# Attention and expert layer on one core: bias tables built from the first score maximum on, half of the last logits summed apart, and transfers that wait for a VectorE operation

## The chip, the core and the metric

The kernel runs on one core of one Trainium2 chip. A core has five engines: TensorE (PE, with its weight loads PEld), VectorE (DVE), ScalarE (ACT), GpSimd (POOL) and SyncE (SP). SP computes nothing here; it issues the DMA transfers, one after the other. The metric is the device time of one execution in microseconds (us), as the median of several runs.

## What is computed

Sliding-window attention with a distance bias for 8 batches of 8 heads, 576 positions and 64 columns, and behind it a layer of 8 experts in which each expert takes at most 80 of the 4608 tokens. Cut to what matters:

```python
# q, k, v: (8, 8, 576, 64)
rel = pos[:, None] - pos[None, :]
scores = q @ k.T / 8 + slope[head] * -abs(rel), where 0 <= rel < 128, else -1e9
attn = exp(scores - max);  x = attn / (sum(attn) + 1e-9) @ v          # tokens 4608 x 512
logits = x @ w_gate                                                  # 512 x 8
expert = argmax(logits);  gate = softmax(logits)[expert]
for e in range(8):                          # the 80 tokens with the largest gate
    out[tok] = gate[tok] * (relu(x[tok] @ w1[e]) @ w2[e])            # 512 x 1024, 1024 x 512
# every other row of out is zero
```

## The kernel before

The program has an attention part and an expert part. The attention part is recorded as operations, put in order by the class `Plan`, and only then issued. That is why nearly all its instructions carry one line, L346, the call in `issue`. `order` (L231) is a list scheduler: it keeps a clock for each engine, estimates each operation's cost, and takes on each engine the ready operation with the smallest key. The key is the place in the program plus the numbers of the table `SHIFT` (L23) for the operation's kind; `SLACK`, `PATIENCE` and `URGENT` say how far it looks ahead and how long TensorE stays in one tile shape. SP's transfers are ordered in the same way. On the chip each engine then runs its own list strictly in order, and waits on semaphores where data or a buffer is missing.

The attention part goes through 80 groups, 10 for each batch. For a group i the steps are: `scores` (TensorE writes the tiles s; VectorE adds the bias table, takes the row's extremum mn and writes e in one custom operation, followed by a read of its accumulator; ScalarE takes the exponential in place), `turned` one group later (TensorE transposes e into pt, VectorE or ScalarE copies it to ptb) and `attend` another group later (TensorE multiplies ptb with the values v into av). A third kind of value column holds a one, so that the last column of av is the sum that the row has to be divided by. `attended` (L781) copies av to xs in SBUF and, after every second pair of heads, writes xs to x_dram in HBM with two transfers.

The bias tables are bneg (tiles of full width), bn (the first tile of a row, masked) and bnx (tiles over two pairs of heads), each a product of a slope sl or slx and the distance rel plus the penalty pen. VectorE builds all of them with `add_bias` (L469) at the program's start. `load_pair` loads q and k of two heads into one of four buffers, `load_vt` a transposed copy of the values for the logits, `load_v` the values with their extra columns. `selection_constants` (L576) makes the tables that the merging below needs, in part on VectorE.

After each batch `merge_steps` (L839) picks the best 80 tokens for each expert among the batch and those kept so far: `norm` takes the reciprocal ztk of the sums, `gate` multiplies the value logits by it (lw), sums over the heads (lg), and goes on with maximum, exponential and selection; `parts` writes the matrix T (ts), `turn` transposes it to m_tp and copies two parts of it to sst (VectorE) and ttt (ScalarE); `diff`, `places` and `keep` (m_d, m_cs, m_gp) count who is ahead of whom. For the last batch nothing lies beside these steps but `keep_clock`, 100 small matmuls (idle_a) without use for the result. The batch in `FAST` does its small steps on VectorE rather than GpSimd.

The expert part is written in plain order. After 10 warm-up matmuls (`warm_up(10, "warm1")`, L1057) `gather` fetches 80 rows of x_dram for each expert, `turn` (L1099) divides them by the sums (rz), scales them by the gate and transposes them; two matrix products h and y follow for each expert. The weights of experts 0 and 1 are loaded during attention, as is the zeroing of out; the others follow the first gathers.

Of the kernel before, what the change touches and what calls it, by code (L numbers as in the profile page):

```python
# [18 lines left out]
P = 128  # L19
# [3 lines left out]
SHIFT = {"idle": 100000, "EXP": 5, "PTB": -45, "AV": 5, "PT": -15, "S": -50, "TTR": 60, "ADD": 80}  # L23
SLACK = 20.0
# [5 lines left out]
class Plan:  # L30
# [17 lines left out]
    DRAIN, PATIENCE, URGENT = 93.0, 150.0, 60  # L48
# [36 lines left out]
    def _labels(self, op, aps):  # L85
        if self.stage == "init":
            return []
# [61 lines left out]
    def add(self, ns_name, eng, name, args, kw):  # L149
# [24 lines left out]
        else:  # L174
            op = _Op(eng, len(self.ops), cost, call)
            op.issue = 450.0 if eng == "SP" and len(outs[0].ap) < 3 else 625.0
            op.lag = 70.0 if name == "tensor_tensor_reduce" else 0.0
# [53 lines left out]
    def order(self, free_order=()):  # L231
# [23 lines left out]
        mode, tick, cols, cold = None, 0, 0.0, True  # L255

# [14 lines left out]
        while len(done) < len(ops):  # L271
# [40 lines left out]
            o.start = t  # L312
            if e == "SP":
                o.end = dma = max(t + self.DMA, dma) + o.cost
                clock[e] = max(t + o.issue, dma - self.DMA)
            else:
                o.end = clock[e] = t + (2 * o.cost if e == "PE" and cold else o.cost)
            done.append(o)
# [22 lines left out]
    def issue(self, tc, free_order=()):  # L341
        done = self.order(free_order)
        with tc.manual_schedule():
            for o in done:
                for c in o.calls:
                    c.ins = c.f(*c.args, **c.kw)  # L346

# [27 lines left out]
def tile_attention_then_moe(  # L375
# [40 lines left out]

    def staged(label, f):
        def run():
            nc.stage = label
            f()  # L420
            nc.stage = None
        return run
# [49 lines left out]
    def make_bias(g):  # L472
        for a_ in range(2):
            add_bias(bneg[:, g, a_], sl[:, g, a_:a_ + 1], rel, pen)
        for a_ in range(2):
# [26 lines left out]
    def load_v(b):  # L502
        for g in range(0, NP, 2):
# [3 lines left out]
        nc.gpsimd.memset(vts[b % 2].rearrange("p g h n c -> p (g h n) c")[:, :, XW - 1:XW], 1.0)  # L507
# [17 lines left out]
    load_pair(0, 1)  # L525
    load_vt(0)
    wg = const.tile([P, NP, 32], F32, name="wg")
    nc.gpsimd.memset(wg, 0.0)
# [8 lines left out]
    load_v(0)  # L537
    load_pair(0, 2)
    nc.vector.memset(zero, 0.0)
# [34 lines left out]
    ztk = [persist.tile([P, NU, H], F32, name=f"ztk{i}") for i in range(2)]  # L574

    def selection_constants():  # L576
# [3 lines left out]
        nc.vector.tensor_copy(pf, pi)  # L580
# [3 lines left out]
        nc.vector.tensor_copy(uf, ui)  # L584
        pb = pf.broadcast_to([P, NU])
        for t in ts:
# [4 lines left out]
            nc.vector.tensor_scalar(t[:, :, 29], pb, EPS, None, ALU.mult)  # L591
            nc.vector.tensor_scalar(t[:, :, 30], uf, EPS, None, ALU.mult)
            nc.vector.tensor_scalar(t[:, :, KS + 27], pb, 0.5, -EPS, ALU.add, ALU.mult)
            nc.vector.tensor_scalar(t[:, :, KS + 28], uf, -EPS, None, ALU.mult)
        bi = const.tile([P, B, NU], I32, name="bi")
        nc.gpsimd.iota(bi, pattern=[[S, B], [P, NU]], base=P, channel_multiplier=0)
        nc.vector.tensor_copy(idc[:, :, 0], bi.rearrange("p b u -> p (b u)"))
        nc.vector.tensor_copy(idc[:, :, 1], pf.broadcast_to([P, B * NU]))
        ii = const.tile([P, R], I32, name="ii")
        nc.gpsimd.iota(ii, pattern=[[-1, R]], base=0, channel_multiplier=0)  # L600
        nc.vector.tensor_copy(itb, ii)
# [16 lines left out]
        nc.vector.tensor_copy(ita, ij)  # L618
        nc.vector.tensor_copy(identb, ident)
# [4 lines left out]
        nc.vector.tensor_copy(wt, wt_i)  # L624
        nc.vector.tensor_copy(wtu, wt.unsqueeze(1).broadcast_to([P, NU, 8]))
        nc.vector.memset(wtu[64:128, NU - 1], -1.0)
# [41 lines left out]
    def value_columns(b):  # L668
        def run():
            lp = ps(f"vw{b}")  # L670
            sel = ident.rearrange("p (g c) -> p g c", g=NP)
            with nc.together():
# [8 lines left out]
            nc.scalar.copy(  # L681
                vts[b % 2][:, :, :, :, D:D + E].rearrange("p g h n e -> p g (h n) e"),
                lp[:, 0:64 * NVP].rearrange("p (m g e) -> p g m e", g=NP, e=E))
# [19 lines left out]
    def scores(i, b, steps):  # L703
# [17 lines left out]
        for s, st in enumerate(steps):  # L721
# [4 lines left out]
            for a_ in range(2):  # L726
# [3 lines left out]
                nc.vector.tensor_tensor_reduce(  # L730
                    x, sps[a_][:, 192 * s + o0:192 * s + 192], bias, -(D ** -0.5), 3.0e38, ALU.add, ALU.min, m)
# [49 lines left out]
    def attended(b, g):  # L781
# [8 lines left out]
        if g % 2:  # L790
            r0, h0 = P + S * b, 2 * g - 2
            xd = x_dram.rearrange("r (h d) -> r h d", d=XW)
# [15 lines left out]
    def gate(b):  # L808
        ve = nc.vector if b in FAST else nc.gpsimd
        lg = small.tile([P, NU, E], F32, tag="lg", name=f"lg{b}")  # L810
        lw = small.tile([P, NU, H, E], F32, tag="lw", name=f"lw{b}")
        zt = ztk[b % 2]
        ve.tensor_tensor(lw, xss[b % 2][:, :, :, D:D + E], zt.unsqueeze(3).broadcast_to([P, NU, H, E]), ALU.mult)
        nc.vector.tensor_reduce(lg, lw.rearrange("p u h e -> p u e h"), axis=AX.X, op=ALU.add)
# [24 lines left out]
    def merge_steps(b):  # L839
# [5 lines left out]
        def parts():  # L845
# [26 lines left out]
            th = small.tile([P, 2, E], BF16, tag="th", name=f"th{b}")  # L872
            for j in range(2 if last else 1):
                ve.tensor_scalar(th[:, j], eq[:, j], 0.5, None, ALU.mult)
            st["th"] = th
# [3 lines left out]
        def turn():  # L879
            tp = psb(f"m_tp{b}")  # L880
            with nc.together():
                for u in range(NU):
# [349 lines left out]
```

## Time and profile before

| what | value |
|---|---|
| median of 3 runs (342.03 to 346.26) | 342.69 us |
| the profiled execution | 342.97 us |
| its span, first to last instruction | 341.2 us |
| mean granted TensorE clock | 0.962 |
| attention part, to the end of the last av | 0 to 227.97 us |
| selection of the last batch, to the first token numbers (gid) | 228.04 to 240.49 us |
| first expert's h to the last y | 246.77 to 335.44 us |
| bytes moved | 98.09 MB |

The profile is one execution, so a sum made from it is held against 342.97 us. Its times count from the span's start. PE matmuls overlap, so that a busy TensorE is not one at its peak; idle time of an engine costs only where that engine is the one that others wait for. "issue" as a releaser means that the engine waited for nothing that the profile shows.

### The profile page before, as it was taken

Reading aid. Unit: us, or ns where it says so; the run is one execution under the profiler, and the core shown is the slowest. Engines: PE = TensorE matmul, PEld = TensorE weight load, DVE = VectorE, ACT = ScalarE, POOL = GpSimd, SP = SyncE. Lnnn points to the kernel's source line nnn. Section 1 sums busy time; section 2 is a strip of 40 time slices with the busy share of each in tenths; the row PEclk is TensorE's granted clock in tenths of the full one; section 3 lists DMA queues with packets and bytes.
Section 4 is the critical chain, followed back from the end, with each engine's and each line's share of the span. In section 5 each row is a group of like instructions: output and inputs, shape, how many; then the busy total and the mean of one; then the engine's idle time right before and its main releaser. Section 6 shows DMA issues by size and latency. Waiting matters only on the chain. (4 is left out here: it accounts for less than half of the span.)

```text
span 341.2 us, 14662 instructions
## 1 busy us (share of the span) xinstructions
PE 310.1 (91%) x6069; PEld 243.9 (71%) x6069; DVE 194.1 (57%) x964; ACT 204.6 (60%) x554; POOL 59.5 (17%) x223
## 2 busy tenths in 40 slices
PE   7399999999999889996988999997679999999993
PEld 6278888888787778795877888896675566655660
DVE  8957667688767687876558787866400122210200
ACT  1469979789958869887576997963003222233221
POOL 7700012022012004013000401200540111100111
PEclk9699999999999999999699999999779999999998
DMA  6995979998989999999499999831299999999300
GB/s 195 343 409 184 345 257 302 355 318 297 349 301 314 318 324 273 337 338 340 134 295 314 315 391 338 326 133 52 75 306 355 399 402 400 395 397 401 133 21 19
DMA packets 44113, 98.09 MB, mean 287 GB/s; under 512 B 4240, under 2 KB 14224, under 8 KB 44048
## 3 DMA queue, kind: packets, MB, share of 16 engines
q1 hardware_dynamic: 43024, 94.36, 79.0%
q0 software_dynamic: 1024, 2.81, 2.7%
q8 instruction: 48, 0.79, 0.9%
q14 instruction: 17, 0.14, 0.1%
HBM read 75.34 MB, written 21.81 MB: 285 GB/s over the span
## 5 line engine op out<-in xcount | busy, mean ns | idle before, releaser
L346 ACT ACTIVATE e<-e,mn 128x192 f32<-128x192 f32 (+1 forms) x288 | 108.4, 437 | 16.0 <-DVE mn L346 15.7
L346 PE MATMUL av<-v,ptb 128*64 128x73 f32 (+1 forms) x2112 | 73.3, 232 | 6.1 <-issue 6.1
L346 PEld LDWEIGHTS av<-v,ptb 128*64 128x64 f32 (+1 forms) x2112 | 64.1, 135 | 17.0 <-issue 12.3
L346 DVE CUSTOM_DVE_ANT_0 e<-s,bneg 128x192 f32<-128x192 f32 x192 | 59.9, 350 | 9.0 <-PE s L346 6.0
L346 PE MATMUL pt<-ident,e 128*128 128x128 f32 x432 | 58.7, 284 | 3.6 <-DVE identb L346 3.6
L346 PE MATMUL s<-kp,q 64*64 64x192 f32 (+1 forms) x1152 | 58.3, 316 | 3.9 <-DVE mn L346 2.5
L346 PEld LDWEIGHTS pt<-ident,e 128*128 128x128 f32 x432 | 48.6, 145 | 10.7 <-POOL e L346 3.9
L346 DVE COPY ptb<-pt 128x384 f32<-128x384 f32 x80 | 43.0, 550 | 15.7 <-PE pt L346 10.3
L1177 DVE TENSOR_TENSOR ys<-ys,y 80x512 f32<-80x512 f32 x8 | 5.5, 684 | 77.6 <-ACT ys L1172 77.6
L346 PEld LDWEIGHTS s<-kp,q 64*64 64x64 f32 x1152 | 40.6, 134 | 8.5 <-issue 4.3
L1147 PEld LDWEIGHTS h<-xgTs,w 128*64 128x64 f32 x1024 | 40.0, 146 | 9.0 <-issue 8.9
L1147 PE MATMUL h<-xgTs,w 128*64 128x80 f32 x1024 | 41.9, 244 | 2.3 <-issue 2.3
L1170 PE MATMUL y<-w,hT 128*32 128x512 f32 (+1 forms) x288 | 42.8, 594 | 0.0
L346 ACT COPY xs<-av 128x584 f32<-128x584 f32 (+1 forms) x64 | 27.9, 462 | 15.3 <-PE av L346 14.0
L346 ACT COPY ptb<-pt 128x384 f32<-128x384 f32 x64 | 30.3, 474 | 8.9 <-PE av L346 4.4
L1170 PEld LDWEIGHTS y<-w,hT 128*32 128x32 f32 (+1 forms) x288 | 10.5, 105 | 24.9 <-issue 24.2
L1152 ACT ACTIVATE hT<-h 128x320 f32<-128x320 f32 x16 | 7.0, 437 | 35.5 <-PE h L1147 35.5
L346 DVE CUSTOM_DVE_ANT_0 e<-s,bn 128x128 f32<-128x128 f32 x64 | 16.1, 286 | 16.1 <-PE s L346 15.1
L346 DVE DVE_READ_ACCUMULATOR2_ANT mn<- 128x1 f32 x288 | 23.8, 82 | 0.0
L1180 POOL DMA_INDIRECT out_dram<-ys,sid x8 | 7.4, 921 | 78.9 <-DVE rz L1104 60.4
L346 DVE TENSOR_SCALAR_CACHE_REDUCE ncm<-m_d 128x80 bf16<-128x80 f32 (+5 forms) x55 | 17.2, 370 | 2.7 <-PE m_d L346 2.5
L346 POOL MEMSET e<- 128x128 f32 x32 | 6.5, 204 | 64.3 <-PE pt L346 58.5
(143 smaller groups left out, 352.0 us busy)
## 6 DMA issues: line engine op xcount, KB each, us to landing
w<-in_moe_w_dram SPq DMA_DIRECT2D x64, 512.0 KB, 10.8
v<-in_v_dram SPq DMA_DIRECT2D x16, 730.0 KB, 6.2
x_dram<-xs SPq DMA_DIRECT2D x16, 584.0 KB, 4.4
l_vt<-in_vt_dram SPq DMA_DIRECT2D x16, 576.0 KB, 7.3
out_dram<-zero SPq DMA_DIRECT2D x18, 512.0 KB, 6.7
kp<-in_k_dram SPq DMA_DIRECT2D x31, 288.0 KB, 4.6
q<-in_q_dram SPq DMA_DIRECT2D x31, 288.0 KB, 6.6
x_dram<-xs SPq DMA_DIRECT2D x16, 73.0 KB, 5.0
```

Of the source, the lines that this page charges most:

```text
L346: c.ins = c.f(*c.args, **c.kw)
L1147: nc.tensor.matmul(hp[64 * hh:64 * hh + 64, R * fi:R * fi + R], lhsT=a[:, cc, f0:f0 + 64], rhs=xgT[:, cc], start=(cc == 0), stop=(cc == NC ...
L1152: nc.scalar.activation(hT[:, 4 * f2:4 * f2 + 4].rearrange("p c r -> p (c r)"), hp[:, 0:4 * R], AF.Relu)
L1170: nc.tensor.matmul(o, lhsT=hT[:, f_, l0:l1], rhs=c[:, f_], start=st, stop=sp)
L1177: nc.vector.tensor_tensor(ys, ys, yp[0:R, 0:DM], ALU.add)
L1180: nc.gpsimd.indirect_dma_start(out=out, out_offset=bass.IndirectOffsetOnAxis(ap=sid[:, e:e + 1], axis=0), in_=ys, in_offset=None, bounds_c ...
```

## The change

Five things change together.

1. The planner's numbers are others (`SHIFT`, `SLACK`, `PATIENCE`, `URGENT`), and so the order on every engine. Operations of the new stage "bias" get the kind I and no shift.
2. Each transfer of the attention part that the plan puts after 14 us gets an extra dependence: SP waits for the last VectorE operation that, by the plan, has ended 0.3 us before.
3. At the start only bneg of the first pair is built ahead of the scores. The other tables follow one by one behind the first score maximum, the selection constants behind group 4 and on GpSimd alone. The gate matrix wg comes padded from the host in one transfer instead of two scattered ones, half of the values is loaded ahead of the second pair of q and k, and the value columns of batch 0 are copied in two halves.
4. The sums are inverted in place in xs for each half of the heads, ahead of the write to x_dram. So the expert part needs no rz. For the last batch the first half's logits are summed while attention still runs, the second half's after it, and the two are added. `turn` of the last batch transposes T twice, into m_tp and m_tq, so that the two copies read different tiles; the halves th are taken in `turn` rather than in `parts`.
5. `warm_up` ahead of the experts has 17 matmuls instead of 10.

```diff
-SHIFT = {"idle": 100000, "EXP": 5, "PTB": -45, "AV": 5, "PT": -15, "S": -50, "TTR": 60, "ADD": 80}
-SLACK = 20.0
+SHIFT = {"idle": 100000, "EXP": 45, "E": 60, "PTB": 15, "TTR": -20, "AV": 15, "M": 60, "S": 35, "XS": -80, "PT": 20}
+SLACK = 0.0
...
+    PACED = 14000.0
+    DRAIN, PATIENCE, URGENT = 93.0, 50.0, 100
...
+            if e == "SP" and t > self.PACED:
+                while len(beat) > 1 and beat[1].end + self.LAT["DVE"]["SP"] <= t:
+                    beat.pop(0)
+                o.pace = beat[0]
...
+                if o.pace is not None:
+                    tc.add_manual_dep(
+                        o.calls[0].ins.ins, o.pace.calls[-1].ins.ins.name,
+                        mybir.DependencyInfo(mybir.DependencyClass.Sync, mybir.DependencyReason.DATA),
+                        reason="a short queue")
...
+    make_bias(0)
     nc.vector.tensor_copy(pen0, pen[:, 64:192])
     nc.vector.memset(pen0[0:64, 0:64], -BIG)
-    make_bias(0)
...
     load_pair(0, 0)
-    load_pair(0, 1)
     load_vt(0)
...
-    for hh in range(2):
-        nc.sync.dma_start(
-            out=wg[64 * hh:64 * hh + 64, :, 8 * hh:8 * hh + 8],
-            in_=w_gate.rearrange("(g hh p) e -> hh p g e", g=NP, hh=2)[hh],
-        )
+    nc.sync.dma_start(out=wg.rearrange("p g c -> p (g c)"), in_=w_gate)
...
-    load_v(0)
+    load_v(0, 0)
+    load_pair(0, 1)
+    load_v(0, 1)
     load_pair(0, 2)
-    nc.vector.memset(zero, 0.0)
...
-        nc.vector.tensor_copy(uf, ui)
+        nc.gpsimd.tensor_copy(uf, ui)
...
-    def norm(b):
-        zt = ztk[b % 2]
+    def norm(b, h0):
         ve = nc.vector if b in FAST else nc.gpsimd
-        ve.tensor_scalar_add(zt, xss[b % 2][:, :, :, XW - 1], 1.0e-9)
-        nc.vector.reciprocal(zt, zt)
+        x = xss[b % 2][:, :, h0:h0 + 4]
+        z = x[:, :, :, XW - 1]
+        with at_stage(f"n{b}"):
+            ve.tensor_scalar_add(z, z, 1.0e-9)
+            nc.vector.reciprocal(z, z)
+
+    def logits(b, h0, n):
+        ve = nc.vector if b in FAST else nc.gpsimd
+        x = xss[b % 2][:, :, h0:h0 + n]
+        lg = small.tile([P, NU, E], F32, tag="lg", name=f"lg{b}_{h0}", bufs=3)
+        lw = small.tile([P, NU, n, E], F32, tag="lw", name=f"lw{b}_{h0}")
+        ve.tensor_tensor(
+            lw, x[:, :, :, D:D + E], x[:, :, :, XW - 1:XW].broadcast_to([P, NU, n, E]), ALU.mult)
+        nc.vector.tensor_reduce(lg, lw.rearrange("p u h e -> p u e h"), axis=AX.X, op=ALU.add)
+        lgs.setdefault(b, []).append(lg)
...
+        logits(b, 4 if b in FAST else 0, 4 if b in FAST else H)
+        lg = lgs[b][-1]
+        if len(lgs[b]) > 1:
+            nc.vector.tensor_tensor(lg, lg, lgs[b][0], ALU.add)
...
-            tp = psb(f"m_tp{b}")
+            tp = tq = psb(f"m_tp{b}")
+            for o in range(2 if last else 1):
+                if o:
+                    tq = psb(f"m_tq{b}")
...
-            for g in range(1, NP):
-                make_slopes(g)
-            for u in range(2):
-                make_cross_slopes(u)
-            make_bias(1)
-            make_cross_bias(0)
...
+            later.extend((
+                lambda: make_start_bias(0), lambda: (make_cross_slopes(0), make_cross_bias(0)),
+                lambda: (make_slopes(1), make_bias(1)), lambda: make_start_bias(1),
...
+                lambda: nc.gpsimd.memset(zero, 0.0)))
+            with nc.after(first[0]):
+                staged("bias", later.pop(0))()
+        for _ in range(2):
+            if later and i:
+                with nc.after(first[0]):
+                    staged("bias", later.pop(0))()
+        if i == 4:
+            with nc.after(first[0]):
+                staged("bias", selection_constants)()
...
-        warm_up(10, "warm1")
+        warm_up(17, "warm1")
...
-        nc.vector.tensor_scalar_add(rz, xg[:, :, XW - 1], 1.0e-9)
-        nc.vector.reciprocal(rz, rz)
```

What this does to the order is shown at three places; the number behind an underscore tells buffers apart. First VectorE at the start. ISA is the custom operation that writes e and mn from a tile s, and behind it the read of the accumulator. Before, these are the last tables and the first maximum:

```order
L346 SCALAR_TENSOR_TENSOR bneg<-rp,sl 128x192 x2
L346 SCALAR_TENSOR_TENSOR bn_84<-rp,sl 128x128 x2
L346 SCALAR_TENSOR_TENSOR bnx<-rp,slx 128x192 x2
L346 ISA e_129,mn_130<-s_0_131,bneg 128x192
L346 ISA mn_130 128x1
```

Now, from the penalty on:

```order
L355 TENSOR_SCALAR rp<-rp_i 128x192
L355 SCALAR_TENSOR_TENSOR bneg<-rp,sl 128x192 x2
L355 COPY rp<-rp 128x128
L355 MEMSET rp 64x64
L355 ISA e_127,mn_128<-s_0_129,bneg 128x192
L355 ISA mn_128 128x1
```

Nine pairs of table operations and a memset of zero have moved from ahead of the first maximum to behind it.

Second SP in the middle of the attention part, at the transfers that follow the second half of batch 5 (xs_120 is its result, v_92 the values of batch 6 or 7, w a piece of expert 1). The brackets name what an instruction waits for: DMAHW is an earlier transfer on the same ring. Before:

```order
L346 DMA x_dram<-xs_120 128x4x292 [waits DMAHW5_49,Activation_49]
L346 DMA x_dram<-xs_120 64x292 [waits DMAHW6_49,Activation_49]
L346 DMA v_92<-in_v_dram 128x1460 [waits DMAHW7_49,PE_49]
L346 DMA kp_89<-in_k_dram 128x576 [waits DMAHW0_49,PE_49]
L346 DMA q_1_688<-in_q_dram 128x576 [waits DMAHW1_49]
L346 DMA kp_90<-in_k_dram 128x576 [waits DMAHW2_49,PE_49]
L346 DMA q_2_715<-in_q_dram 128x576 [waits DMAHW3_49]
L346 DMA w_1_128<-in_moe_w_dram 128x2x512 [waits DMAHW4_49]
```

Now:

```order
L355 DMA v_92<-in_v_dram 128x1460 [waits DVE_49,DMAHW2_49,PE_49,Pool_49]
L355 DMA x_dram<-xs_120 128x4x292 [waits DMAHW3_49,DVE_49,Activation_49]
L355 DMA x_dram<-xs_120 64x292 [waits DMAHW4_49,DVE_49,Activation_49]
L355 DMA kp_88<-in_k_dram 128x576 [waits DMAHW5_49,DVE_49,PE_49]
L355 DMA q_0_668<-in_q_dram 128x576 [waits DMAHW6_49,DVE_49]
L355 DMA kp_89<-in_k_dram 128x576 [waits DMAHW7_49,DVE_49,PE_49]
L355 DMA q_1_687<-in_q_dram 128x576 [waits DMAHW0_49,DVE_49]
L355 DMA kp_90<-in_k_dram 128x576 [waits DMAHW1_49,DVE_49,PE_49]
L355 DMA q_2_718<-in_q_dram 128x576 [waits DMAHW2_49,DVE_49]
L355 DMA w_1_126<-in_moe_w_dram 128x2x512 [waits DMAHW3_49,DVE_49]
```

The run of transfers is as long as before, but each has a VectorE operation of its own to wait for, and the values come ahead of the write of xs.

Third VectorE behind the last av, where xs_121 is the last batch's result. Before:

```order
L346 TENSOR_SCALAR ztk_124<-xs_121 128x40
L346 RECIPROCAL ztk_124<-ztk_124 128x40
L346 TENSOR_TENSOR lw_935<-xs_121,ztk_124 128x320
L346 TENSOR_REDUCE lg_934<-lw_935 128x40
L346 TENSOR_REDUCE mx_936<-lg_934 128x5
```

Now:

```order
L355 TENSOR_SCALAR xs_121<-xs_121 128x5x4
L355 RECIPROCAL xs_121<-xs_121 128x5x4
L355 TENSOR_TENSOR lw_4_935<-xs_121 128x160
L355 TENSOR_REDUCE lg_4_934<-lw_4_935 128x40
L355 TENSOR_TENSOR lg_4_934<-lg_4_934,lg_0_898 128x40
L355 TENSOR_REDUCE mx_936<-lg_4_934 128x5
```

The first four operations work on half as many elements, and one addition comes between the sum and the maximum. The halves th stay where they were in VectorE's list, ahead of kk.

More of the change, by code (lines that the diff above doesn't have):

```diff
@@ L317, in order @@
                 o.end = clock[e] = t + (2 * o.cost if e == "PE" and cold else o.cost)
+            if e == "DVE":
+                beat.append(o)
             done.append(o)
@@ L415, in tile_attention_then_moe, with at_stage @@
     x_dram = dram.tile([P + NTOK, H * XW], F32, name="x_dram")
+    @contextmanager
+    def at_stage(label):
+        old, nc.stage = nc.stage, label
+        yield
+        nc.stage = old
     def staged(label, f):
@@ L500, in tile_attention_then_moe, with load_v @@
     vtt = {}
-    def load_v(b):
-        for g in range(0, NP, 2):
+    def load_v(b, half=None):
+        for g in range(0, NP, 2) if half is None else (2 * half,):
             nc.sync.dma_start(
@@ L617, in selection_constants @@
         nc.gpsimd.iota(ij, pattern=[[1, R]], base=0, channel_multiplier=-1)
-        nc.vector.tensor_copy(ita, ij)
-        nc.vector.tensor_copy(identb, ident)
+        nc.gpsimd.tensor_copy(ita, ij)
+        nc.gpsimd.tensor_copy(identb, ident)
         nc.gpsimd.memset(at, 0.0)
@@ L680, in run @@
                                 lhsT=lx[:, x:x + 64], rhs=sel[:, :, 8 * hh:8 * hh + 8], start=True, stop=True)
-            nc.scalar.copy(
-                vts[b % 2][:, :, :, :, D:D + E].rearrange("p g h n e -> p g (h n) e"),
-                lp[:, 0:64 * NVP].rearrange("p (m g e) -> p g m e", g=NP, e=E))
+            w = NP if b else NP // 2
+            for g in range(0, NP, w):
+                nc.scalar.copy(
+                    vts[b % 2][:, g:g + w, :, :, D:D + E].rearrange("p g h n e -> p g (h n) e"),
+                    lp[:, 0:64 * NVP].rearrange("p (m g e) -> p g m e", g=NP, e=E)[:, g:g + w])
         return run
@@ L729, in scores @@
                 x = e[:, s, a_, o0:]
-                nc.vector.tensor_tensor_reduce(
-                    x, sps[a_][:, 192 * s + o0:192 * s + 192], bias, -(D ** -0.5), 3.0e38, ALU.add, ALU.min, m)
+                first.append(nc.vector.tensor_tensor_reduce(
+                    x, sps[a_][:, 192 * s + o0:192 * s + 192], bias, -(D ** -0.5), 3.0e38, ALU.add, ALU.min, m))
                 nc.scalar.activation(x, x, AF.Exp, bias=m, scale=-1.0)
@@ L871, in parts @@
                 idc[:, NU * b:NU * b + NU].unsqueeze(3).broadcast_to([P, NU, 2, E]), ALU.mult)
[L872 to L875, printed above, removed]
             if last:
@@ L879, in turn @@
         def turn():
-            tp = psb(f"m_tp{b}")
-            with nc.together():
-                for u in range(NU):
-                    nc.tensor.transpose(tp[:, P * u:P * u + P], T[:, u], identb)
-                nc.tensor.transpose(tp[:, S:S + R], at, identb[0:R, 0:R])
-            nc.vector.tensor_copy(sT[0:KS], tp[0:KS, 0:NU * P])
+            tp = tq = psb(f"m_tp{b}")
+            for o in range(2 if last else 1):
+                if o:
+                    tq = psb(f"m_tq{b}")
+                with nc.together():
+                    for u in range(NU):
+                        nc.tensor.transpose(tq[:, P * u:P * u + P], T[:, u], identb)
+                    nc.tensor.transpose(tq[:, S:S + R], at, identb[0:R, 0:R])
             nc.scalar.copy(tT[0:KS], tp[KS:2 * KS, 0:S + R])
+            nc.vector.tensor_copy(sT[0:KS], tq[0:KS, 0:NU * P])
             st["a1"] = small.tile([P, 2], F32, tag="a1", name=f"a1_{b}")
             st["nc"] = ncm
+            th = small.tile([P, 2, E], BF16, tag="th", name=f"th{b}")
+            for j in range(2 if last else 1):
+                ve.tensor_scalar(th[:, j], st["eq"][:, j], 0.5, None, ALU.mult)
+            st["th"] = th
         def diff(pieces):
@@ L982, in tile_attention_then_moe @@
     nc.stage = None
+    later = []
+    first = []
     zeros = []
@@ L1003, in finish_group @@
             attended(b, g)
+            if b in FAST and g == 1:
+                staged(f"n{b}", lambda: logits(b, 0, 4))()
             if g == NP - 1:
@@ L1199, in _layout @@
     a['vt'] = a['vt'].transpose(0, 2, 1, 3).reshape(B, 128, -1)
+    w = a['moe_w_gate'].reshape(H // 2, 2, D, E).transpose(1, 2, 0, 3)
+    wg = _np.zeros((2, D, H // 2, 32), w.dtype)
+    for h in range(2):
+        wg[h, :, :, E * h:E * h + E] = w[h]
+    a['moe_w_gate'] = wg.reshape(128, -1)
     v = a['v'].reshape(B, H // 2, 2, S // 64, 64, D)
```

55 lines of the change are left out of this document (25 added, 30 removed).

## The prediction

> **What bounds the kernel now.** I read the page first, then what TensorE waits for in the attention part, then that part in stretches, and last the start and the selection in order of time. The chain that ended last holds only the final write of the output, so it does not help.
>
> ```profile
> span 341.2 us, 14662 instructions
> PE 310.1 (91%) x6069; PEld 243.9 (71%) x6069; DVE 194.1 (57%) x964; ACT 204.6 (60%) x554; POOL 59.5 (17%) x223
> q8 instruction: 48, 0.79, 0.9%
> ```
>
> TensorE is busy for 91% of the span. Its waits from 20 to 228 us (line waited for: us in total, times, longest) are:
>
> ```profile
> PE av L346 <- issue: 6.1, 4, 2.9
> PE m_gp L346 <- issue: 2.3, 2, 1.4
> PE m_cs L346 <- issue: 1.4, 2, 1.0
> PE s L346 <- issue: 0.7, 2, 0.5
> PE m_tp L346 <- issue: 0.3, 1, 0.3
> ```
>
> So in the steady part it hardly waits for another engine, but 10.8 us (the sum) for nothing that the profile names. The stretches between the ends of such stalls say what it is (columns: us, then each engine's busy time and count, the granted clock, DMA share, GB/s):
>
> ```profile
> 64.50:69.60 5.10, 4.83 (x127) 4.20 (x127) 4.10 (x22) 4.22 (x14) 0.20 (x1) 1.00 0.94 342
> 118.70:125.80 7.10, 5.70 (x125) 5.07 (x125) 5.75 (x27) 4.11 (x12) 0.41 (x2) 1.00 0.89 327
> 125.80:137.00 11.20, 10.97 (x251) 9.19 (x250) 7.97 (x44) 10.54 (x33) 3.55 (x13) 1.00 0.94 292
> 162.30:177.60 15.30, 14.26 (x250) 12.40 (x250) 8.67 (x47) 10.21 (x27) 0.37 (x2) 0.81 0.66 212
> ```
>
> From stall to stall TensorE runs 250 to 254 instructions, or twice as many. The 48 packets of the instruction queue carry 0.79 MB, 16 KB each, and TensorE's 12138 instructions over 48 are 253. So these stalls are late loads of TensorE's own instructions. The largest one shows what made it late:
>
> ```profile
> 151.61 0.93 SPq L346 DMA_DIRECT2D x_dram<-xs  x2
> ...
> 157.74 0.43 SPq L346 DMA_DIRECT2D w<-in_moe_w_dram  x1
> 162.36 0.40 PE L346 MATMUL av<-v,ptb 64*64 64x73 f32 x3 [2.90 <-issue]
> 158.00:160.00 2.00, 1.46 (x48) 1.23 (x45) 1.34 (x10) 2.00 (x7) 0.59 (x4) 1.00 1.08 351
> v<-in_v_dram SPq DMA_DIRECT2D x16, 730.0 KB, 6.2
> q<-in_q_dram SPq DMA_DIRECT2D x31, 288.0 KB, 6.6
> SPq L346 <- ACT xs L346: 51.3, 15, 9.1
> ```
>
> SP, which waits 51.3 us for xs copies, then issues eight transfers in 6.6 us: 3.1 MB (584+73+730+4x288+512 KB). The DMA engines take 351 GB/s, that is 2.3 MB in that time, and are fully busy. The instruction load is then behind by some us. Landing times of 6 to 7 us for transfers that need 1 to 2 us at this rate say the same.
>
> **The change, part by part.** *Start.* VectorE builds tables until 9.00, though scores are there from 5.73:
>
> ```profile
> 4.85 0.88 PE L346 MATMUL s<-kp,q 64*64 64x192 f32 x16
> 8.34 0.74 DVE L346 SCALAR_TENSOR_TENSOR bnx<-rp,slx 128x192 f32<-128x192 f32 x2
> 9.00 0.35 DVE L346 CUSTOM_DVE_ANT_0 e<-s,bneg 128x192 f32<-128x192 f32 x1
> 10.17 2.90 DVE L346 CAST uf<-ui 128x5 f32<-128x5 int32 x1
> 13.81 0.29 DVE L346 CUSTOM_DVE_ANT_0 e<-s,bn 128x128 f32<-128x128 f32 x1
> 14.81 1.51 PE L346 MATMUL pt<-ident,e 128*128 128x128 f32 x6 [3.61 <-DVE identb L346]
> 22.10 1.24 PE L346 MATMUL av<-v,ptb 128*64 128x73 f32 x30
> 0.00:14.00 14.00, 7.72 (x76) 6.22 (x76) 12.93 (x48) 2.77 (x5) 11.84 (x77) 0.90 0.75 240
> 14.00:30.00 16.00, 15.18 (x292) 11.86 (x296) 10.18 (x63) 12.67 (x35) 1.41 (x10) 0.88 0.89 349
> ```
>
> The first maximum comes 3.3 us earlier, and the constants that held VectorE from 10.17 to 13.81 go to GpSimd, where they delay only the memsets of e behind them. The tables are still to be built, but between the first maxima. What is late next is the data. At 240 GB/s the first 2.6 MB (pair 0, the transposed values, gate, half of v) are there at 11 us, pair 1 (0.59 MB more) at 13.3; the rest of v and pair 2 at 349 GB/s from 14 us at about 17.3. So the first av can start at about 12.5. Before, at its start (22.10) TensorE had done besides the scores of groups 2 to 4 and the transposes of 2 and 3: 0.44+0.88+0.88 us (group 2 has half the tiles) and, at the 14.81 row's price for one group, 0.75+1.5 us, 4.5 in all. The new order reaches that point at 17.0: 5.1 us less. Bounds: 0, if TensorE waits for loads instead, and 7.9, all its idle time in the first 14 us (14.00-7.72 = 6.3) plus 1.6 for the 3.2 us from 14.81 that it worked at half clock (0.90 and 0.88 over these stretches are 6.7 us at half clock). I take 5, by the transfer rate.
>
> *Paced transfers.* Worth at most the 10.8 us, plus what the long stall did to the clock: 162.30 to 177.60 took 15.3 us for 500 instructions, of which 1.0 is the next stall, against 11.2 for 501 at clock 1.00; so 3. At least 0, if waiting does not shorten the queue. Between 0 and 13.8 I take three quarters, 10: the waits spread the eight transfers above over VectorE's progress, and what remains is short bursts. [...]
>
> The price of pacing is what waits behind SP's waiting instruction: every later load. A pair of q and k is issued three pairs ahead, and a pair lasts (228-22)/32 = 6.4 us, so there are 19 us for a landing of 6.6; each load has some 12 us to lose before TensorE waits. A write of xs also waits for the reciprocal now; it is needed only by the gather. Below nothing I see no way. Above, the other engines come closer to the bound when TensorE no longer stalls. I take 2 us for waits that take the stalls' place, a fifth of the gain, and as bounds 0 and 10.
>
> *Selection of the last batch.* All of it is on the path:
>
> ```profile
> 229.41 0.40 DVE L346 RECIPROCAL ztk<-ztk 128x40 f32<-128x40 f32 x1
> 229.85 0.49 DVE L346 TENSOR_TENSOR lw<-xs,ztk 128x320 f32<-128x320 f32 x1
> 230.38 0.73 DVE L346 TENSOR_REDUCE lg<-lw 128x40 f32<-128x320 f32 x1
> 231.38 0.20 DVE L346 TENSOR_TENSOR sh<-lg,mx 128x40 f32<-128x40 f32 x1
> 234.19 0.48 DVE L346 COPY sst<-m_tp 32x640 bf16<-32x640 bf16 x1 [0.66 <-PE m_tp L346]
> 234.70 0.70 ACT L346 COPY ttt<-m_tp 32x656 bf16<-32x656 bf16 x1 [2.09 <-DVE sst L346]
> 244.71 0.17 DVE L1104 TENSOR_SCALAR rz<-xg 80x8 f32<-80x8 f32 x1 [3.61 <-DMA xg<-x_dram,gid]
> 245.15 0.88 DVE L1108 SCALAR_TENSOR_TENSOR xn<-xg,gwf,rz 80x256 f32<-80x256 f32 x2
> ```
>
> Half the elements save about 0.14 + 0.17 + 0.32 (the fixed part of each read off sh, 0.20 for 40 elements); the added sum costs 0.20 and a gap of 0.04; so 0.4. With two transposed tiles the ScalarE copy starts at 234.19 beside VectorE's; but the second transpose adds about 0.5 us ahead of sst, so only 0.25 is left of the serial 0.5. Moving th gains nothing, its place is the same. Without rz the first xn starts 0.44 earlier, for the later experts it is hidden by h and y. Sum 1.1, between 0.6 and 1.6. The first half's logits lie in the attention part beside TensorE: a few operations of VectorE, nothing.
>
> *Seven more warm-ups.*
>
> ```profile
> 240.11 3.96 PE L439 MATMUL warm<-const-float32-0.0 128*128 128x128 f32 x20
> 247.00:248.00 1.00, 1.00 (x18) 1.00 (x18) 0.14 (x1) 0.00 (x0) 0.98 (x1) 0.50 0.86 229
> 246.77 3.63 PE L1147 MATMUL h<-xgTs,w 128*64 128x80 f32 x50 [0.34 <-issue]
> 263.00 4.75 PE L1147 MATMUL h<-xgTs,w 128*64 128x80 f32 x128
> ```
>
> The first h runs at half clock: 50 instructions in 3.63 us, against 1.86 at the later rate of 4.75 for 128. The 14 extra instructions end at about 245.5 at full clock (0.1 each), 246.8 at half; TensorE is needed at 245.5. So the bounds are a loss of 1.3 and a gain of 1.8 for these 50, or 3.5 if the rest of this h goes at full clock too. I take a gain of 1.5.
>
> *Sum.* 342.97 - 5 - 10 + 2 - 1.1 - 1.5 = 327.4; the profiled run stands 0.3 above the median, so 327.
>
> **Rivals.** *Pacing does not help.* The extra waits are met when SP gets there (it waits 51 us for xs alone anyway), or the instruction load does not stand behind SP's transfers. For this: nothing in the profile shows the queue it stands in. Against it: every stall lies in a stretch with the DMA engines at 0.9 or more. Then 342.97-5-1.1-1.5 = 335.4. [...]
>
> *No gain at the start*: the loads, not the tables, set it. For: 0.75 to 0.89 DMA share there. Against: 13.81, where VectorE alone was late. 332.4.
>
> *Slower*: SP's waits make each load late. If the slack of 12 us is used up, each of 31 pairs makes TensorE wait; at 0.9 us per pair that adds 28, so 355. It decides from 0.72 us per pair on (22.4 us to reach +2%). Against it: the slack.
>
> **How the numbers follow.** Forecast 0.62, pacing without gain 0.18, no gain at the start 0.12, slower 0.08. The forecast's own bounds reach from 319 (13.8 and 7.9 taken whole and 1.5 of the new waits gone: 327.4-3.8-2.9-1.5) to 335 (10 us of new waits instead of 2); with the first two rivals 319 to 338 holds more than 8 in 10, and the slower case stays out. Faster by over 2% means under 335.8; 2% is about what a measurement of this kernel can tell from no change: 0.62 of the forecast nearly whole, 0.11 and about half of 0.18, so 0.80; within 2%, 0.13; slower 0.07.
>
> **What would show it.** The first maximum near 5.8 us and the first av near 12.5; TensorE's "issue" waits from 20 to 228 us at 2 to 4 us instead of 10.8, without a half-clock stretch after 160; new waits of TensorE for DMA of at most 2; the last av about 13 us earlier; from the last av to the first gather 0.7 us less; the first h at full clock. It would be wrong if the issue waits stay, or if waits for kp, q or v appear in their place.

## The result, and the profile after

| | median us (runs) | ratio to before |
|---|---|---|
| before | 342.36 (340.46 to 346.26, 4) | |
| changed | 328.15 (326.97 to 329.29, 4) | 0.9602, 95% 0.9544 to 0.9661 |
| changed, the profiled execution | 328.23 | its span 326.5 |

The change makes the kernel 3.98% faster. The prediction was 327.0 in a range of 319 to 338; its sum, 327.4, stands 0.8 below the profiled execution. Ratios here and below leave disturbed runs out, medians do not, so where the two differ the ratio counts.

The page of the changed kernel, for the rows that answer to those of before:

```profile
span 326.5 us, 14835 instructions
PE 308.4 (94%) x6086; PEld 241.9 (74%) x6089; DVE 185.5 (57%) x941; ACT 201.7 (62%) x555; POOL 67.9 (21%) x256
```

TensorE has 1.7 us less busy time (308.4 against 310.1), so the 14.7 us of the span are mostly idle time that is gone. What TensorE waits for from 20 to 228 us (line waited for: us in total, times, longest):

```profile
PE s L355 <- ACT ptb L355: 1.6, 2, 1.1
PE m_gp L355 <- DVE oa L355: 1.3, 1, 1.3
PE m_tp L355 <- POOL ts L355: 1.1, 1, 1.1
PE l L355 <- DMA l_vt<-in_vt_dram: 0.5, 1, 0.5
PE m_d L355 <- issue: 0.5, 3, 0.2
PE av L355 <- issue: 0.5, 1, 0.5
PE pt L355 <- ACT ptb L355: 0.4, 2, 0.2
...
PE pt L355 <- issue: 0.3, 1, 0.3
```

Issue waits are 1.3 us instead of 10.8 (the m_gp row lies in the last batch's selection, behind the attention part). Those for ScalarE, GpSimd and DMA come to 3.6 in the attention part (1.6+0.4, 1.1 and 0.5). The stretches of the changed kernel (us, then busy time and count of PE, PEld, DVE, ACT, POOL, granted clock, DMA share, GB/s) show full clock where before had 0.90, 0.88 and, from 162.30 to 177.60, 0.81:

```profile
0.00:14.00 14.00, 11.69 (x160) 9.58 (x164) 9.47 (x41) 6.13 (x14) 9.55 (x64) 1.00 0.82 291
14.00:30.00 16.00, 15.63 (x336) 12.82 (x328) 13.24 (x78) 13.80 (x39) 8.99 (x45) 1.00 0.94 322
150.00:180.00 30.00, 29.14 (x672) 24.90 (x668) 23.08 (x132) 25.86 (x77) 6.13 (x26) 1.00 0.96 325
```

The value logits l come once for each batch, so they mark the progress. The rows of batch 1 and batch 7, first of before and then of the changed kernel, in the order of time:

```profile
34.76 1.18 PE L346 MATMUL l<-l_vt,wg 128*32 128x288 f32 x16
...
199.68 1.18 PE L346 MATMUL l<-l_vt,wg 128*32 128x288 f32 x16
```

```profile
6.41 0.36 DVE L355 CUSTOM_DVE_ANT_0 e<-s,bneg 128x192 f32<-128x192 f32 x1 [2.82 <-PE s L355]
12.84 1.15 PE L355 MATMUL av<-v,ptb 128*64 128x73 f32 x32
28.95 0.68 PE L355 MATMUL l<-l_vt,wg 128*32 128x288 f32 x4
...
183.69 1.18 PE L355 MATMUL l<-l_vt,wg 128*32 128x288 f32 x16
```

The first maximum and the first av come 2.6 and 9.3 us earlier; at batch 1, where TensorE has run about as many instructions in both, 5.8 are left. A batch then takes 25.79 us ((183.69-28.95)/6) instead of 27.49. Behind the last av the changed kernel shows:

```profile
213.66 1.10 ACT L355 COPY xs<-av 128x584 f32<-128x584 f32 x3 [1.77 <-PE av L355]
...
225.23 6.79 PE L459 MATMUL warm<-const-float32-0.0 128*128 128x128 f32 x34
225.45 0.17 DVE L1109 TENSOR_REDUCE gid<-m_gp 80x8 uint32<-80x16 f32 x1 [0.68 <-PE m_gp L355]
...
229.87 0.88 DVE L1150 SCALAR_TENSOR_TENSOR xn<-xg,gwf 80x256 f32<-80x256 f32 x2 [3.65 <-DMA xg<-x_dram,gid]
...
232.23 0.47 PE L1161 MATMUL xgT<-ident,xn 80*128 80x80 f32 x4 [0.21 <-issue]
233.06 1.71 PE L1189 MATMUL h<-xgTs,w 128*64 128x80 f32 x36 [0.36 <-ACT xgTs L1162]
235.20 0.28 PE L1189 MATMUL h<-xgTs,w 128*64 128x80 f32 x1 [0.42 <-issue]
235.92 0.23 PE L1189 MATMUL h<-xgTs,w 128*64 128x80 f32 x1 [0.44 <-issue]
236.65 0.30 PE L1189 MATMUL h<-xgTs,w 128*64 128x80 f32 x2 [0.50 <-issue]
237.39 0.30 PE L1189 MATMUL h<-xgTs,w 128*64 128x80 f32 x2 [0.44 <-issue]
238.12 4.75 PE L1189 MATMUL h<-xgTs,w 128*64 128x80 f32 x86 [0.43 <-issue]
```

The copy of the last av starts 14.38 us earlier than before (228.04). From it to the first xn it takes 16.21 us (229.87-213.66) instead of 17.11. Then the gain stops: the 34 warm-up matmuls take 6.79 us (0.2 each), run at half clock (granted 0.50) until 231 and end at 232.0, while the first half of xn is done by about 230.3; and the first h idles 2.2 us in pieces between 234.8 and 238.1 (0.42+0.44+0.50+0.44+0.43) and then runs at half clock for some 3.3 us (granted 0.52 from 238.1 to 241.4). The first h of before idled 1.9 us in the same way (the issue waits at 251.51, 252.23 and 252.95). From the first xn to the end the changed kernel takes 96.6 us (326.5-229.87), before 96.1 (341.2-245.15).

So of 14.7 us, 5.8 come from the start, 8.6 from the rest of the attention part, 0.9 from the selection and the first xn, and some 0.6 are lost at the warm-ups and the first h.

### The profile page after: what moved, and what is told of

Read it like the earlier page. It is cut to its first block, busy times and chain, and to the rows that moved or that the text cites. A ratio compares the mean times of both kernels' runs of the same rounds, so it can differ in the third digit from the quotient of the medians.

```text
span 326.5 us, 14835 instructions
## 1 busy us (share of the span) xinstructions
PE 308.4 (94%) x6086; PEld 241.9 (74%) x6089; DVE 185.5 (57%) x941; ACT 201.7 (62%) x555; POOL 67.9 (21%) x256
## 5 line engine op out<-in xcount | busy, mean ns | idle before, releaser
L355 ACT ACTIVATE e<-e,mn 128x192 f32<-128x192 f32 (+1 forms) x288 | 105.5, 436 | 10.3 <-DVE mn L355 10.2
L355 PE MATMUL av<-v,ptb 128*64 128x73 f32 (+1 forms) x2112 | 72.5, 232 | 0.5 <-issue 0.5
L355 PEld LDWEIGHTS av<-v,ptb 128*64 128x64 f32 (+1 forms) x2112 | 61.8, 134 | 14.5 <-issue 9.0
L355 DVE CUSTOM_DVE_ANT_0 e<-s,bneg 128x192 f32<-128x192 f32 x192 | 59.0, 350 | 16.4 <-PE s L355 13.3
L355 PE MATMUL s<-kp,q 64*64 64x192 f32 (+1 forms) x1152 | 54.4, 313 | 1.7 <-ACT ptb L355 1.6
L355 PEld LDWEIGHTS pt<-ident,e 128*128 128x128 f32 x432 | 46.5, 141 | 7.7 <-issue 2.4
L1189 PEld LDWEIGHTS h<-xgTs,w 128*64 128x64 f32 x1024 | 38.5, 141 | 9.5 <-issue 8.9
L1189 PE MATMUL h<-xgTs,w 128*64 128x80 f32 x1024 | 40.6, 239 | 2.6 <-issue 2.2
L1212 PEld LDWEIGHTS y<-w,hT 128*32 128x32 f32 (+1 forms) x288 | 10.5, 105 | 24.9 <-issue 24.2
L1222 POOL DMA_INDIRECT out_dram<-ys,sid x8 | 9.0, 1120 | 77.6 <-DVE ys L1219 77.6
L1212 PE MATMUL yx_d<-w,hT 128*32 128x512 f32 x32 | 15.2, 598 | 0.0
```

What stands on the lines that cost most here:

```text
L1189: nc.tensor.matmul(hp[64 * hh:64 * hh + 64, R * fi:R * fi + R], lhsT=a[:, cc, f0:f0 + 64], rhs=xgT[:, cc], start=(cc == 0), stop=(cc == NC ...
L1212: nc.tensor.matmul(o, lhsT=hT[:, f_, l0:l1], rhs=c[:, f_], start=st, stop=sp)
L1222: nc.gpsimd.indirect_dma_start(out=out, out_offset=bass.IndirectOffsetOnAxis(ap=sid[:, e:e + 1], axis=0), in_=ys, in_offset=None, bounds_c ...
```

## Experiments

The kernels of one group ran on one chip beside the kernel before, so ratios are compared inside a group. The kernel before took 338.06 us in the first group, 336.86 in the second and 343.87 in the third.

| group | kernel | median us (range) | ratio, 95% |
|---|---|---|---|
| 1 | changed, unpaced | 329.81 (327.56 to 334.11) | 0.979, 0.965 to 0.993 |
| 1 | before, paced | 333.93 (328.63 to 337.72) | not settled |
| 1 | changed, old tables | 328.48 (327.97 to 330.95) | 0.979, 0.967 to 0.991 |
| 1 | changed, late weights | 325.31 (321.52 to 329.54) | 0.964, 0.951 to 0.977 |
| 2 | changed again | 323.19 (320.11 to 328.87) | 0.955, 0.948 to 0.962 |
| 2 | changed, unpaced again | 329.23 (325.56 to 332.65) | 0.973, 0.966 to 0.981 |
| 2 | changed, old numbers | 336.83 (331.42 to 339.84) | 0.985, 0.975 to 0.994 |
| 2 | changed, 10 warm-ups | 325.23 (324.26 to 325.78) | 0.964, 0.957 to 0.970 |
| 3 | changed, third time | 329.37 (327.6 to 331.58) | 0.964, 0.957 to 0.970 |
| 3 | changed, bursts of 4 | 374.03 (368.23 to 379.64) | 1.092, 1.082 to 1.101 |
| 3 | before, new numbers | 340.67 (338.43 to 345.12) | 0.993, 0.989 to 0.997 |
| 3 | changed, late weights, 13 warm-ups | 329.33 (326.86 to 334.59) | 0.960, 0.953 to 0.967 |

### Pacing alone, in the new order and in the old

```diff
-    PACED = 14000.0
+    PACED = 1.0e9
```

> The changed kernel without the dependence of transfers on VectorE; every engine's order is the same as in the changed kernel. If pacing is what shortened the instruction loads' wait (theory): the issue waits of TensorE between 20 us and the last av return to 8 to 11 us from 1.3, the new waits for ACT, POOL and DMA (3.6 us) partly go, and the time is 334 to 338 us. If the new order alone did it (rival): issue waits stay under 3 us and the time is 326 to 330 us.

> The changed kernel without the dependence of transfers on VectorE, five rounds beside the changed kernel. If pacing is worth most of the 10 us that the prediction gave it: 6 to 10 us above the changed kernel on the same chip. If the new order and start do most of it: 0 to 4 us above.

> The changed kernel once more, on the chip of the three runs beside it: the reference for them. Theory (pacing shortens the wait for instruction loads): issue waits from 20 us to the last av again 1 to 3 us, and the time again 0.955 to 0.966 of before. Rival (the 1.3 us of the first profile were luck, since the same list of instructions stood at 6.8 us in the kernel with late weights): 4 to 8 us of issue waits, ratio 0.966 to 0.98.

In the second group the unpaced kernel stands 1.9% above the changed one (0.9732 against 0.9549), about 6 us, and by the two intervals between 3 and 10: the lower edge of what was expected of pacing, and not quite clear of the 0 to 4 us of the rival. In the first group it stands 1.5% above the kernel with late weights, whose attention part is the changed one's, and there the intervals overlap. Its issue waits are 8.5 us, 10.0 in the first group; the changed kernel in the same order shows 1.3, 4.4 and 3.0 in its three profiles. The three kernels below that differ from it in the expert part alone show 1.1, 2.2 and 7.2. So the 1.3 of the first profile was in part luck: the repeat's 4.4 lies where the rival had it, its ratio where the theory had it. What the waits are is seen best instruction by instruction. TensorE's long issue waits, first unpaced, then in the changed kernel of the same group, then in that of the third group (start, duration, operation; the bracket has the idle time before it):

```profile
24.59 0.59 PE L355 MATMUL s<-kp,q 64*64 64x128 f32 x9 [1.12 <-issue]
...
114.77 1.07 PE L355 MATMUL av<-v,ptb 128*64 128x73 f32 x33 [2.83 <-issue]
...
168.60 0.54 PE L355 MATMUL av<-v,ptb 64*64 64x73 f32 x19 [1.48 <-issue]
181.22 1.41 PE L355 MATMUL pt<-ident,e 128*128 128x128 f32 x11 [1.44 <-issue]
```

```profile
25.33 0.59 PE L355 MATMUL s<-kp,q 64*64 64x128 f32 x9 [1.12 <-issue]
...
114.21 1.07 PE L355 MATMUL av<-v,ptb 128*64 128x73 f32 x33 [1.45 <-issue]
178.94 1.41 PE L355 MATMUL pt<-ident,e 128*128 128x128 f32 x11 [0.96 <-issue]
```

```profile
24.62 0.59 PE L355 MATMUL s<-kp,q 64*64 64x128 f32 x9 [1.12 <-issue]
42.77 0.66 PE L355 MATMUL pt<-ident,e 128*128 128x128 f32 x4 [0.81 <-issue]
```

The stalls stand at the same instructions, so they belong to the places where a new load of instructions begins. The traces hold the loads themselves, and these show it directly. The one ahead of the 2.83 us stall runs on the instruction queue from 112.32 to 113.24, and TensorE resumes at 114.77, 1.5 us behind its end. In seven profiles (before, before with pacing, the unpaced kernel in two groups, the changed one in three) all 38 issue waits of 0.4 us or more between 20 us and the last av end 1.2 to 1.6 us after such a load has ended. The load itself takes about 1 us, 2 at the longest, with a stall as without, so what is late is mostly its start.

The stall before av x33 falls from 2.83 to 1.45 and in the third run under 0.5, that before pt x11 from 1.44 to 0.96 and under 0.5, though only the moments at which SP issues differ. The one before s x9 is the same 1.12 with pacing as without. So pacing shortens the sum, as the prediction had it, but not every stall, and how long each is varies from one execution to the next.

The other half of the test puts the dependence into the kernel before:

```diff
+            if e == "SP" and t > self.PACED:
+                while len(beat) > 1 and beat[1].end + self.LAT["DVE"]["SP"] <= t:
+                    beat.pop(0)
+                o.pace = beat[0]
```

> The kernel before with the dependence of transfers on VectorE alone; every engine's order is the same as before. Theory: issue waits from 20 to 228 us fall from 10.8 to 1 to 4 us, no half-clock stretch after 160 us, time 331 to 335 us. Rival (the new order is what helps): issue waits stay near 10 us, time 341 to 345 us.

Between the two: the issue waits from 20 to 228 us are 9.0 us and the clock from 160 to 180 us is 0.91, so a half-clock stretch is still there. That is the rival's side; but the median falls by 4.1 us, without a settled ratio. The same places, first before and then with pacing:

```profile
177.61 0.42 PE L346 MATMUL m_cs<-ts,ncm 128*128 128x8 bf16 x11 [0.99 <-issue]
184.23 0.18 PE L346 MATMUL m_gp<-ts,ob 128*80 128x54 bf16 x1 [0.97 <-issue]
```

```profile
164.43 0.34 PE L355 MATMUL av<-v,ptb 64*64 64x73 f32 x4 [1.95 <-issue]
178.29 0.42 PE L355 MATMUL m_cs<-ts,ncm 128*128 128x8 bf16 x11 [0.57 <-issue]
184.63 0.18 PE L355 MATMUL m_gp<-ts,ob 128*80 128x54 bf16 x1 [0.70 <-issue]
```

Each is about a third shorter here too (the first stood at 2.90 before), but others have come up elsewhere, so the sum hardly moves. By the issue waits, then, pacing does less in the old order than in the new. The time of a batch in the profiles (value logits of batch 1 to batch 7) says the same: 27.38 us instead of 27.49 in the old order, 25.55 to 26.58 in six profiles instead of 26.46 and 27.18 in the new one. The times of whole runs do not show it: in this group the medians give 4.1 us in the old order and 4.5 in the new one (329.81 against 325.31 with late weights).

### The planner's numbers

```diff
-SHIFT = {"idle": 100000, "EXP": 45, "E": 60, "PTB": 15, "TTR": -20, "AV": 15, "M": 60, "S": 35, "XS": -80, "PT": 20}
-SLACK = 0.0
+SHIFT = {"idle": 100000, "EXP": 5, "PTB": -45, "AV": 5, "PT": -15, "S": -50, "TTR": 60, "ADD": 80}
+SLACK = 20.0
...
-    DRAIN, PATIENCE, URGENT = 93.0, 50.0, 100
+    DRAIN, PATIENCE, URGENT = 93.0, 150.0, 60
```

> The changed kernel with the planner's numbers of before (SHIFT, SLACK, PATIENCE, URGENT), start and pacing new. The prediction gave the numbers no term of their own. If it was right in that: within 1.5 us of the changed kernel. If the new numbers carry part of the gain (rival): 3 to 6 us above it, with TensorE's waits for ScalarE or VectorE, not for issue, larger.

The rival holds, and by more than it asked: 3.1% above the changed kernel (0.9846 against 0.9549), 10 us, and by the two intervals between 6 and 14. Only its last part fails, since issue waits have grown as well. TensorE's three largest waits with the old numbers:

```profile
PE s L355 <- issue: 4.1, 2, 2.1
PE m_tp L355 <- POOL ts L355: 2.8, 3, 1.6
PE av L355 <- issue: 2.3, 4, 0.8
```

Issue waits are 7.3 us against 4.4 in the changed kernel beside it, waits for GpSimd 3.9 against 0.7, those for ScalarE fall from 1.9 to 0.7; and the granted clock is 0.88 in the first 14 us and 0.94 from 60 to 90, where the changed kernel has 1.00, which is 3.5 us of work. Together some 8 of the 11.8 us by which the last av is later (229.31 against 217.53 for the copy behind it). The rest I could not place.

The reverse, the new numbers alone in the kernel before (the tables of the start kept unshifted):

> The kernel before with the planner's numbers of the changed one (SHIFT, SLACK, PATIENCE, URGENT), start, transfers and selection as before, the start's tables unshifted as before. If the numbers carry a gain of their own (what the run with the old numbers suggests, 0.985 against 0.955): 5 to 9 us faster than before, 25.8 us or less from batch to batch. If they only pay together with pacing and the new start (rival): within 3 us of before, 26.2 us from batch to batch.

The rival again: 0.7% faster, 2.4 us (1 to 4 by the interval). A batch takes less (26.58 us from batch 1 to 7, before 27.49), but the selection constants and tables still hold the start, and issue waits are 7.9 us. So the numbers are worth 2.4 us by themselves and 10 with the other parts in place.

### The start

The tables go back ahead of the first maximum and the constants to VectorE; the order of the loads stays new.

```diff
-            later.extend((
...
-                staged("bias", selection_constants)()
+        if i == 1:
+            staged("init", lambda: (make_bias(2), make_start_bias(2), make_bias(3), make_start_bias(3),
+                                    make_cross_bias(1)))()
+            staged("init", selection_constants)()
```

> The changed kernel with the bias tables and zero on VectorE ahead of the first maximum and the selection constants on VectorE behind group 1, as before; the order of the loads stays new. If the tables set the start (theory): first maximum at 9 to 10 us, first av at 16 to 20 us instead of 12.8, time 331 to 334 us. If the loads set it (rival): first av stays within 1.5 us of 12.8 and the time is 327 to 330 us.

The first maximum and the first av:

```profile
8.78 0.35 DVE L355 CUSTOM_DVE_ANT_0 e<-s,bneg 128x192 f32<-128x192 f32 x1
16.69 1.83 PE L355 MATMUL av<-v,ptb 128*64 128x73 f32 x56
```

Both are where the theory put them; the median, 328.48, is in the rival's range. But this chip was faster than that of the first runs. By the ratio the kernel stands 1.5% above the one with late weights in its group, whose attention part is the changed one's: 5 us, with intervals that overlap. In the two profiles, though, the copy of the last av starts at 220.99 with the old tables and at 221.94 with late weights, so nothing of the late start is left there. That the tables delay the first av is shown by the rows; what this costs in the end is not settled between 0 and 5.

### Warm-ups and the first h

```diff
-        warm_up(17, "warm1")
+        warm_up(10, "warm1")
```

> The changed kernel with 10 warm-up pairs instead of 17. If the warm-ups are worth the 1.5 us of the prediction: the first h takes about 6.3 us instead of 4.65 and the time is 1 to 2 us above the changed kernel. If their length cancels what the clock gives (rival, from the first profile of the changed kernel, where xgT waited for the warm-ups until 232.0 us though xn was ready at 230.7): within 0.7 us of it.

The first h of this kernel, then that of the changed kernel beside it:

```profile
233.09 7.01 PE L1189 MATMUL h<-xgTs,w 128*64 128x80 f32 x128 [0.23 <-ACT xgTs L1162]
```

```profile
236.53 4.65 PE L1189 MATMUL h<-xgTs,w 128*64 128x80 f32 x128 [0.36 <-ACT xgTs L1162]
```

Each pair is two matmuls in the trace, so the kernel before has 20 and the changed one 34. The seven pairs make this h 2.36 us shorter and let it start 0.94 later behind the first token numbers (7.22 us behind gid instead of 6.28). That is 1.4 us, as predicted, and the ratios (0.964 and 0.955) agree within their intervals. It is one pair of profiles: the 34 matmuls took from 4.04 us (unpaced, second group, 0.12 each, in a profile with a mean granted clock of 0.995) to 6.79 (0.20 each). From gid to the first y the kernels with 17 pairs and no stall take 11.0 to 12.4 us, the one with 10 pairs 13.6. In this group no h stalls.

For the stall that the first profiles show inside this h, the weights of experts 2 and 3 were the suspect: the DMA share is 1.04 from 234.8 to 238.1 us. They are issued behind the first half of h instead:

```diff
-                piece().ins, first.ins.name,
+                piece().ins, act.ins.name,
```

> The changed kernel with the weights of experts 2 and 3 issued after the first half of the first h instead of after the second gather. If the stalls inside the first h (234.5 to 238.1 us, 0.4 us at a time, no engine named) are instruction loads or reads held up by these weights (theory): they vanish, the half-clock stretch behind them too, and the time is 323 to 326 us. If they belong to the code itself (rival): same stalls, 327.5 to 329.5 us; later experts' waits for their weights would show the price, at most 2 us.

> The changed kernel with the weights of experts 2 and 3 issued behind the first half of the first h, and 13 warm-up pairs instead of 17. If the warm-ups end when the first tokens are there and the clock stays full: first xgT about 1 us earlier, first h at 4.65 us, no stall in it, and the time 0.5 to 1.5 us below the changed kernel, 3 to 5 us where that one shows the stall in the first h. If 13 pairs are too few for the clock (rival): first h at 6 to 7 us and 0.5 to 1.5 us above it.

The first of the two says nothing, because on its chip no kernel stalls there. The second ran where the changed kernel does stall. Its first h:

```profile
237.83 0.38 PE L1182 MATMUL h<-xgTs,w 128*64 128x80 f32 x4 [1.03 <-issue]
239.26 0.37 PE L1182 MATMUL h<-xgTs,w 128*64 128x80 f32 x5 [1.05 <-issue]
240.69 4.56 PE L1182 MATMUL h<-xgTs,w 128*64 128x80 f32 x65 [1.06 <-issue]
```

SP issues the weights behind it, and from 230 to 241 us the only DMA queue at work is that of the gathers (packets, MB, share of the engines):

```profile
241.48 8.09 SPq L663 DMA_DIRECT2D w<-in_moe_w_dram  x11
```

```profile
q0 software_dynamic: 499, 1.48, 49.6%
```

The stall is there without any weight in flight, and without a load on the instruction queue. So the suspicion falls, and with it the gain: 0.960 against 0.964, the same. Only the first xgT comes earlier, as expected (5.30 us behind gid instead of 6.49 in the changed kernel beside it). The stall shows in the first two profiles and in all four of the third group, in none of the eight others, whichever kernel it was; the gathers run beside the first h in all fourteen. What makes it was not found.

For the changed kernel of that group a ratio of 0.949 to 0.966, 1 to 7 us of issue waits and 24.9 to 25.4 us for a batch had been expected. It came to 0.964 and 3.0, but 25.55 for a batch, just outside.

### Bursts, and late loads

All transfers of a burst of up to four wait for what the last of them waited for.

```diff
+            if burst and (o is None or len(burst) == 4 or o.start > burst[0].start + 8000.0):
...
+                for x in burst:
+                    x.pace = burst[-1].pace
```

In this kernel one load of values (the first half of batch 5) comes behind the memset of its column of ones, so that these sums are not formed; nothing else is left out.

> The changed kernel with every engine's order kept, but paced transfers gathered in bursts of up to four: all of a burst wait for the VectorE operation that the last of them waited for, so that they are issued one right behind the other. If pacing helps because it breaks bursts (theory): issue waits of TensorE back at 7 to 11 us and the time 4 to 8 us above the changed kernel, like without pacing or worse. If it helps because transfers start later as such (rival): same as the changed kernel within 2 us.

Neither: 44 us above the changed kernel, with 5.0 us of issue waits up to the last av. The large waits, of all engines, are now others:

```profile
POOL v L365 <- DMA v<-in_v_dram: 76.2, 11, 12.0
...
DVE eq L365 <- POOL sh L365: 18.8, 5, 5.7
...
PE s L365 <- ACT ptb L365: 9.8, 2, 5.3
```

GpSimd waits 76.2 us for the loads of the values (36.3 in the changed kernel of the same group), because the memset of the ones stands behind each load in its list; the selection steps and the memsets of e queue up behind that, VectorE and ScalarE behind these. A batch takes some 32 us instead of 25.55, so that at 253 instructions a load the loads come a fifth less often, by an estimate from these numbers, and the run cannot tell whether bursts bring their stalls back. What it shows is the price of lateness.

## Why the prediction was right, and where it was not

**What bounds the kernel** held: the issue waits are late instruction loads, at fixed instructions, and shorter when SP's transfers are spread. The issue waits fell further than the 2 to 4 us that were named (1.3; in six profiles of this order 1.1 to 7.2), the wait for DMA is 0.5, the half-clock stretch behind 160 us is gone, and the last av came 14.4 us earlier instead of 13. Only the first h did not run at full clock.

**Start, -5.** 5.8 us at batch 1 in the first profile, 3.6 in the third group's (value logits at 31.12) and 2.3 in the second's (32.44), all against the one profile of before. With the planner's old numbers the changed kernel has them at 30.48, 4.3 earlier. The first maximum came at 6.41 instead of 5.8 and the first av at 12.84 instead of 12.5, so the transfer rate placed it well. The tables' own part is between 0 and 5.

**Paced transfers, -10, and new waits, +2.** Taking pacing away costs 6 us (3 to 10) against the net 8 of the sum. The waits that took the stalls' place are 3.6 us in the first profile, but the unpaced kernels have 1.4 and 1.8 of these too (for ScalarE and VectorE); pacing's own are about 2. In the new order the issue waits are 1.1 to 7.2 us with pacing, in six profiles, and 8.5 and 10.0 without it; before they were 10.8.

**Selection, -1.1.** 0.9 from the copy of the last av to the first xn, of which 0.5 lies ahead of the first gather, where 0.7 had been expected.

**Seven more warm-ups, -1.5.** The mechanism is right (the first h takes 4.65 us behind 17 pairs, 7.01 behind 10) and worth 1.4 us where nothing else stalls. In the profiled pair it brought nothing: from gid to the first y 17.77 us (243.22-225.45) instead of 17.39 (257.71-240.32), 0.8 worse when the 0.44 without rz are counted. The 1.5 lay near the bound at full clock, estimated at 0.1 us for each extra matmul; until 231 us they ran at half clock (0.50, and 0.2 us each), near the other bound, and the first h stalled anyway, with half clock (0.52) behind the stall again.

**What failed** is a step that the prediction did not take: the planner's numbers got no term, and the other terms were priced in the order of before and added. With the old numbers the start, pacing, selection and warm-ups together bring 1.5% (0.9846), 5 us (2 to 8), where the sum had 15.6; the new numbers bring the other 10, though alone in the kernel before they bring 2.4. So the parts do not add up. Why they do not is shown in part only: by the issue waits and the time of a batch pacing merely moves the stalls in the old order (9.0 instead of 10.8; 27.38 us for a batch, and 27.47 with the old numbers in the changed kernel, instead of 27.49), and in the new one it removes most of them, but the times of whole runs do not tell the two apart. That the sum came out within 1 us is in part luck: a missing term of 10 us stood against terms that were too large by as much in the order in which they were priced.

**Rivals.** That pacing does not help is wrong in the new order; in the old it is not settled. The argument against it, that every stall lies where the DMA engines are busy at 0.9 or more, was weak: the changed kernel's stretches have 0.94 to 0.98 from 14 to 180 us, with hardly a stall, and in the kernel before the share is 0.27 from 44.2 to 46.7 us, where a stall of 0.46 us ends. That the start gains nothing is wrong. That late loads make it slower does not happen in this change, but the bursts of four show that it is near: loads held back by up to 8 us of the plan's time cost 44 us, and not through TensorE's waits for q and k, as the rival had it, but through GpSimd's list behind the loads of v.

**Open** are the stall inside the first h, some 4 us of the difference that the numbers make, what makes a load of instructions start late while SP's transfers are queued, and whether another way to spread them would do as well. No version that was run beats the changed kernel beyond its interval.

## What to carry to other kernels

Where an engine waits for nothing that the profile names, count its instructions from stall to stall, and look for a packet of the instruction queue that ends just ahead of each. Equal counts pointed to loads of the engine's own code here, the packets confirmed it, and spreading SP's transfers shortened the sum. Price a change of order together with what it meets: the planner's numbers were worth 2.4 us alone and 10 in company. Before transfers are held back, look for the small operations that stand behind a load in another engine's list.

## What the runs showed of the hardware

One list of attention instructions has from 1.1 to 7.2 us of issue waits in six profiles, and the changed kernel's runs on one chip spread from 320.11 to 328.87. In seven profiles, each with 48 loads of instructions of 16 KB (0.79 MB), TensorE resumed 1.2 to 1.6 us after the end of such a load at all 38 stalls of 0.4 us or more. Warm-up matmuls on a busy TensorE ran at a granted clock of 0.50 from 225 to 231 us, 6 us long, before it rose to 1.00 (changed kernel); in the kernel before from 240 to 243. In the unpaced kernel of the second group the same 34 took 4.04 us instead of 6.79. A product with data and weights in SBUF was held up in six of fourteen profiles, a few matmuls at a time, over 2.5 to 4 us, 1.7 to 3.1 of them idle; in those of the kernel before, the changed kernel and late weights with 13 warm-ups no packet ran on the instruction queue q8 meanwhile.
